# x by an identity product in PSUM, first scores on 256 tokens, other packing of score rounds, a new order

## The chip, the cores and the metric

The kernel runs on one core of one Trainium2 chip. The metric is the device time of one execution in microseconds; where several runs are shown, their median. TensorE is called PE here, VectorE DVE, ScalarE ACT, GpSimd POOL; SP only issues DMAs.

## The reference, cut to what matters

x has 2048 tokens of width 512. Attention with a compressive memory and a gated MLP follow each other twice, each with a layer norm ahead of it and x added behind it. Attention works in 4 segments of 512 tokens, on 32 heads of width 16: a causal softmax inside the segment, mixed by sigmoid(beta) with a read of a memory M that the segments before it have filled.

```python
def _A_ref(x, wq, wk, wv, wo, beta):
    ...
    for s in range(N):                      # 4 segments of 512 tokens
        p = _softmax(qs @ ks.T * scale + mask)
        a_dot = p @ vs
        num, den = phi(qs) @ M, phi(qs) @ z + 1e-6
        o = g * num / den + (1 - g) * a_dot
        M, z = M + phi(ks).T @ vs, z + sum(phi(ks))
    return o @ wo

def _B_ref(x, w_gate, w_up, w_down):        # width 1792
    return _gelu(x @ w_gate) * (x @ w_up) @ w_down

x = x + _A_ref(_layernorm(x), ...)
x = x + _B_ref(_layernorm(x), ...)
x = x + _A_ref(_layernorm(x), ...)
x = x + _B_ref(_layernorm(x), ...)
```

## The kernel before

**Units of work.** Two passes of four segments make eight units, k = 0 to 7. Each unit has an attention part (`Att`) and an MLP part (`Ffn`). A segment is four tiles of 128 tokens. Weights and x stay in SBUF; PSUM has eight banks of 512 columns.

**Attention of a unit.** Four tiles of x are normed: bn_stats and bn_aggr on DVE (L514, L522), the power -1/2 on POOL for all four tiles at once (L527, L532), the scaling to xn on DVE or POOL (L544). xn is transposed into xnT, for k = 0, 1, 2 by PE through PSUM (a "turn", L586, copied out at L461 or L462), otherwise by a DMA. Then q, k and v are projected, blocks of four matmuls of 512 columns (L476 or L471). The scores of a group of four head pairs b and of a half of them (par 0 or 1) are packed into rounds of 256 columns (`FULL`), nine rounds for each b, the fifth being shared by both halves (`PAIRED`). A round has matmuls of 64, 192 or 256 columns on row tiles (L938). Two rounds at a time fill two pairs of banks; ACT takes the exponential of a pair (L1396) into the buffer pt; POOL masks the diagonal blocks of a round (L1343, `DIAG` says how many 64-column blocks), the shared round is masked by DVE (L1353) or by POOL in halves (L1348). A "flush" (L954) multiplies the five rounds of a half with v on column tiles, 40 matmuls; DVE turns and scales its result (L971 to L986). k is also copied with half of the heads set to zero (kx, L417, L422), which the odd half needs.

**Memory and MLP.** phi of q and k go through ACT, POOL and DVE (L741, L764, L745); k's is transposed by DMA. The projection wo is 16 matmuls, and DVE adds its result to x in SBUF (L1027). The norm of the sum is turned by PE for k = 0, 1 and 7 (`BY_PE`). Then 14 gate blocks of four matmuls (`gate`), gelu on ACT, 14 blocks `up` with a product on DVE (L1092), and `down`, 14 matmuls for each of four tiles, added to x again.

**What sets the order.** All engines run an order that is written out when the program is built: `order` keeps a clock for every engine (`Clocks`, `Engine`), with a cost written beside each instruction, and picks the next instruction of PE by due times and of the others by slacks. The numbers of this choice stand in `POLICY`; `CHANGES`, which can replace them in each stretch of 20 us, is empty. Where no item is ready while scores are left, PE gets a product of a constant tile, `warm`, whose result nobody reads (L476 or L471), called filler here. Ahead of each turn of a norm in `BY_PE` stand two such products of half width:

```python
            fill = FILL if self.key in BY_PE else 0
            ops = [(Clocks.MM[512] / 2, whole(lambda: nc.tensor.matmul(
                ps()[:, half:L], lhsT=warm[:], rhs=wide[:, 0:2, :], start=True, stop=True)))] * fill
```

A matmul of 512 columns can be issued whole (`128*128`, L476) or as four of 128*32 on column tiles (L471, `product`). PE is thus in one of three modes, whole, rows (scores) and columns (flushes and what is issued between them); `product` stays in column mode where a flush is near, so as to change mode less.

**The head, written out by hand.** 15 products of `warm` (L349) run first. Four tiles of x are loaded, then on ACT's queue beta, broadcast to 128 partitions, and on SP's queue wk and wq in halves of 256 columns. The first norm is computed tile by tile (L1183 to L1193, L544) and turned (L596), ACT copies two turned tiles and DVE two (`first_turn`, L599, L601); ACT takes two exponentials of beta ahead of its copies (L1202, L1203). The first k and q blocks are computed in halves of 256 tokens (`first_k` L909, `first_q` L914), all four halves ahead of the first two score rounds.

**The end.** The last unit's `down` adds to x, and SP stores each tile.

## Time and profile before

| | us |
|---|---|
| median of 3 runs | 546.09 (545.96 to 546.21) |
| profiled execution | 545.75 |
| its span, first to last instruction | 544.0 |

The table of stages below is the answer on busy time by stretch: from and to in us, its length, and for each engine the busy us and the number of instructions; then the granted share of PE's clock and the share of the DMA engines.

```profile
0.00:14.00 14.00, 11.41 (x83) 5.79 (x85) 9.78 (x31) 8.30 (x16) 6.64 (x17) 1.00 0.83 251
14.00:34.00 20.00, 19.53 (x293) 10.20 (x296) 18.56 (x45) 19.79 (x29) 17.40 (x21) 1.00 0.27 74
68.00:136.00 68.00, 67.11 (x1236) 34.86 (x1243) 63.24 (x120) 60.15 (x74) 46.29 (x51) 1.00 0.25 53
476.00:544.00 68.00, 64.66 (x628) 33.67 (x624) 33.22 (x58) 13.36 (x20) 2.43 (x3) 0.99 0.05 17
```

The columns after the length are PE, PEld (weight loads, which run beside matmuls), DVE, ACT and POOL. A matmul's row is longer than the time by which it holds up the next one, so busy PE is read from the starts of its matmuls, not from the sum of its rows. In the two early stretches DVE and ACT are also nearly full; in the last one there are no scores left, and PE works alone but for evictions and products.

Some rows of groups that the text uses (line, engine, operation, out<-in, shapes, count, busy us and mean ns of one, idle time ahead of it and who ended it):

```profile
L1396 ACT ACTIVATE pt<-ps 128x1024 bf16<-128x1024 f32 x288 | 278.9, 1025 | 44.6 <-PE ps L938 41.1 <-POOL pt L1343 2.5 <-POOL kx L417 0.2
L1343 POOL TENSOR_SCALAR_AFFINE_SELECT pt<-pt 128x256 bf16<-128x256 bf16 x128 | 60.2, 483 | 51.4 <-ACT pt L1396 45.5 <-PE ps L938 4.7
L1343 POOL TENSOR_SCALAR_AFFINE_SELECT pt<-pt 128x512 bf16<-128x512 bf16 x64 | 47.7, 745 | 66.6 <-ACT pt L1396 66.5
L532 POOL TENSOR_TENSOR rs<-ve,mhalf 128x4 f32<-128x4 f32 x15 | 16.4, 1092 | 1.2
```

### The profile page before, as it was taken

What the parts mean: (1) busy time and instruction counts of PE and PEld (TensorE: products, weight loads), DVE (VectorE), ACT (ScalarE), POOL (GpSimd) and SP (SyncE); (2) the same over time, 40 slices, a digit from 0 to 9 for tenths busy, and PEclk for the clock granted to TensorE, in tenths of its full rate; (3) what the DMA queues carried; (4) which work ended last, traced back from release to release, by engine and by line L of the source; (5) the groups of instructions that cost most, each with busy time, mean ns of one, the idle gap of its engine ahead of it and who ended that gap; (6) DMA issues with size and microseconds to landing.
All of it is one profiled execution on the core that took longest, in us unless ns stands there. A gap on an engine that the chain in (4) does not pass through costs nothing.

```text
span 544.0 us, 21276 instructions
## 1 busy us (share of the span) xinstructions
PE 531.3 (98%) x9273; PEld 276.3 (51%) x9334; DVE 443.7 (82%) x816; ACT 434.7 (80%) x540; POOL 305.5 (56%) x359
## 2 busy tenths in 40 slices
PE   8999999999999999999999999999999999999997
PEld 4454555454545444554545555545465456555444
DVE  6998999799988999779987998889586797786342
ACT  5999989988898989989899798996879977920330
POOL 4898786369746788339993468716753265300000
PEclk9999999999999999999999999999999999999999
DMA  8406511610331123310312250221320114100001
GB/s 249 117 13 192 118 20 13 176 33 22 45 56 21 26 40 58 44 40 7 41 32 49 33 72 3 41 32 23 78 52 3 22 21 82 24 3 22 19 0 40
DMA packets 64926, 26.95 MB, mean 50 GB/s; under 512 B 49216, under 2 KB 64832, under 8 KB 64832
## 3 DMA queue, kind: packets, MB, share of 16 engines
q1 hardware_dynamic: 64400, 25.31, 22.6%
q8 instruction: 73, 1.20, 0.9%
q10 hardware_dynamic: 432, 0.27, 0.2%
q14 instruction: 21, 0.17, 0.1%
HBM read 9.71 MB, written 2.10 MB: 22 GB/s over the span
## 4 chain that ended last, share of the span: by engine, by line
PE 88%; DVE 7%; DMA 2%; issue 2%; ACT 0%; ACTq 0%; SPq 0%; DVEq 0%
PE ps L476 46%; PE ps L471 26%; PE ps L938 8%; PE ps L954 7%; DVE st L514 1%; DVE x_sb L1027 1%; DMA beta_bc<-in_A_beta_dram 1%; DVE byq L971 1%; PE ps L586 1%; DVE phiq L745 1%; PE ps L584 1%; DMA phik<-e 0%; DMA amT<-am 0%; DVE xn L544 0%; DVE e L764 0%
## 5 line engine op out<-in xcount | busy, mean ns | idle before, releaser
L1396 ACT ACTIVATE pt<-ps 128x1024 bf16<-128x1024 f32 x288 | 278.9, 1025 | 44.6 <-PE ps L938 41.1
L1343 POOL TENSOR_SCALAR_AFFINE_SELECT pt<-pt 128x256 bf16<-128x256 bf16 (+1 forms) x192 | 107.0, 571 | 118.0 <-ACT pt L1396 112.0
L1092 DVE TENSOR_TENSOR gel_sb<-gel_sb,ps 128x512 bf16<-128x512 bf16 x112 | 75.3, 682 | 33.9 <-PE ps L476 25.0
L476 PE MATMUL ps<-xnT,wu_sb 128*128 128x512 bf16 x287 | 66.8, 379 | 1.4 <-issue 1.1
L476 PE MATMUL ps<-xnT,wg_sb 128*128 128x512 bf16 x261 | 62.6, 379 | 0.9 <-issue 0.5
L764 POOL TENSOR_SCALAR e<-e 128x512 bf16<-128x512 bf16 x37 | 57.9, 1565 | 1.8 <-ACT e L741 0.7
L971 DVE STREAM_TRANSPOSE byq<-ps 128x512 f32<-128x512 f32 x64 | 45.0, 706 | 16.5 <-PE ps L954 15.9
L476 PE MATMUL ps<-wd_sb,gel_sb 128*128 128x512 bf16 (+1 forms) x293 | 56.8, 340 | 1.3 <-issue 1.0
L1348 POOL TENSOR_SCALAR_AFFINE_SELECT pt<-pt 64x1024 bf16<-64x1024 bf16 x40 | 47.8, 1196 | 15.0 <-ACT pt L1396 13.7
L1027 DVE TENSOR_TENSOR x_sb<-x_sb,ps 128x512 bf16<-128x512 bf16 (+1 forms) x68 | 42.8, 640 | 16.3 <-PE ps L476 14.7
L471 PE MATMUL ps<-wd_sb,gel_sb 128*32 128x512 bf16 (+1 forms) x792 | 47.1, 378 | 0.3 <-issue 0.3
L476 PEld LDWEIGHTS <-wu_sb 128*128 128x128 bf16 x301 | 28.2, 98 | 33.8 <-issue 0.7
L471 PE MATMUL ps<-xnT,wg_sb 128*32 128x512 bf16 x700 | 42.4, 380 | 0.0
L514 DVE BATCH_NORM_STATS2 st<-x_sb 128x6 f32<-128x512 bf16 x60 | 40.4, 674 | 0.4 <-DMA x_sb<-in_A_x_dram 0.3
L476 PEld LDWEIGHTS <-wg_sb 128*128 128x128 bf16 x273 | 25.3, 98 | 28.8 <-issue 0.2
L476 PEld LDWEIGHTS <-gel_sb 128*128 128x128 bf16 x306 | 28.3, 98 | 22.7 <-issue 1.1
L954 PE MATMUL ps<-pt,vaug 128*32 128x256 bf16 (+2 forms) x1344 | 34.6, 238 | 0.0
L417 POOL TENSOR_SCALAR kx<-kf,masks 128x512 bf16<-128x512 bf16 x20 | 33.5, 1678 | 1.2
L471 PE MATMUL ps<-xnT,wu_sb 128*32 128x512 bf16 x588 | 34.1, 379 | 0.0
L1151 ACT ACTIVATE gel_sb<-gel_sb 128x2048 bf16<-128x2048 bf16 (+1 forms) x21 | 33.2, 1643 | 0.0
L544 DVE TENSOR_SCALAR xn<-x_sb,mv,rs 128x512 bf16<-128x512 bf16 x58 | 31.3, 592 | 2.2 <-POOL rs L532 1.9
L954 PEld LDWEIGHTS <-vaug 128*32 128x32 bf16 x1344 | 27.8, 97 | 10.4 <-issue 2.2
(147 smaller groups left out, 883.6 us busy)
## 6 DMA issues: line engine op xcount, KB each, us to landing
vz<-vaug SPq DMA_DIRECT2D x14, 136.0 KB, 2.9
wg_sb<-in_B_w_gate_dram SPq DMA_DIRECT2D x8, 224.0 KB, 4.6
wu_sb<-in_B_w_up_dram SPq DMA_DIRECT2D x8, 224.0 KB, 4.3
wd_sb<-in_B_w_down_dram SPq DMA_DIRECT2D x7, 256.0 KB, 4.2
x_sb<-in_A_x_dram SPq DMA_DIRECT2D x3, 512.0 KB, 7.3
out_dram<-x_sb SPq DMA_DIRECT2D x12, 128.0 KB, 1.8
xnT<-xn SPq DMA_TRANSPOSE x40, 2.5
wk_sb<-in_A_wk_dram SPq DMA_DIRECT2D x2, 256.0 KB, 6.0
```

The lines of the kernel that those rows point to most:

```text
L471: nc.tensor.matmul(out[r], lhsT=lhsT[:, r], rhs=rhs, start=start, stop=stop, tile_position=(0, 32 * c))
L476: nc.tensor.matmul(out, lhsT=lhsT, rhs=rhs, start=start, stop=stop)
L514: nc.vector.bn_stats(out=self.st6[:, 0, :], in_=x_sb[:, self.tt0 + j, :])
L764: lambda eng: eng.tensor_scalar(out=e[0][:], in0=e[0][:], scalar1=1.0, scalar2=None, op0=ALU.min), summed)
L938: nc.tensor.matmul(ps_all[:, bank, o + c0:o + c0 + n], lhsT=lhsT, rhs=self.q[rows, b, q0:q0 + n], start=True, stop=True, tile_position=(32 ...
L954: nc.tensor.matmul(ps()[32 * j:32 * j + 32, q0:q0 + n], lhsT=va[:, ki * VW + g:ki * VW + g + 32], rhs=pt_all[:, places[i], j, c0:c0 + n], ...
L971: nc.vector.transpose(out=self.byq[:, par, :, :].rearrange("p a c -> p (a c)"), in_=ps()[:])
L1027: ck.dve.post(ck.made(), slack, (0.15 + 0.00104 * (c1 - c0), lambda: nc.vector.tensor_tensor(out=xt, in0=xt, in1=ps()[:, 0:c1 - c0], op=AL ...
L1092: ck.dve.post(ck.made(), NORMAL, (0.683, lambda: nc.vector.tensor_tensor(out=g, in0=g, in1=ps()[:], op=ALU.mult), lambda t: (ps.read(t), e ...
L1343: nc.gpsimd.affine_select(out=view, in_=view, pattern=[[0, 4], [0, n], [1, C]], compare_op=ALU.is_ge, fill=0.0, base=C, channel_multiplier=-1)
L1348: nc.gpsimd.affine_select(out=view, in_=view, pattern=[[0, 4 * TPS], [1, C]], compare_op=ALU.is_ge, fill=0.0, base=0, channel_multiplier=-1)
L1396: nc.scalar.activation(out=pt_all[:, s0:s0 + 2, 2 * p:2 * p + 2, :].rearrange("p r h c -> p h r c"), in_=ps_all[:, pair[0]:pair[1] + 1, :] ...
```

## The change

- **Order and policy.** `POLICY` has other values, and `CHANGES` now holds values for each of 28 stretches of 20 us; the planner's costs of DMA issues and POOL instructions are changed, and so the order of nearly everything is new. FILL is gone; `pol.fill`, which takes its place, is 0 everywhere. One more input norm (`pe_turns` 3 for 2) is turned by PE.
- **x in PSUM.** For units k < `pol.x_pe`, `wo` begins with a product of the identity and x, so that the sum stands in PSUM; bn_stats reads it there, and an eviction writes x.
- **Norm and gates.** The norm ahead of the MLP is scaled in two groups of two tiles; the first four gate blocks of each unit (`split`) are computed in halves of 256 tokens, the first half as soon as two tiles are turned. The first `wo` block (`wsplit`) is issued without its last matmul, which follows when the last attention tile is there.
- **Rounds.** `FULL` packs the first two rounds otherwise, `DIAG` is [2, 0, 0, 2] for [1, 1, 0, 2], and `ORDER` gives the rounds of each b another sequence; two rounds that need the same mask get it in one POOL instruction. In unit 0 two pairs of banks that lie side by side share one exponential (`join`), and evictions, gelus and products of neighbouring banks can be joined (`Mate`).
- **Head.** beta is loaded as one row and brought to all partitions by a product with ones; 13 products of `warm`; the first two score rounds need 256 tokens alone and are issued ahead of the second halves of q and k (`first_scores`).

```diff
-WARM = 15
+WARM = 13
...
-FULL = [[(0, 64, 256, 0)], [(1, 192, 64, 0), (0, 320, 192, 64)], [(1, 256, 256, 0)], [(3, 448, 64, 0), (2, 320, 192, 64)]]
-DIAG = [1, 1, 0, 2]
-SHARED = len(FULL)
+FULL = [[(1, 192, 64, 0), (0, 64, 192, 64)], [(0, 256, 256, 0)], [(1, 256, 256, 0)], [(3, 448, 64, 0), (2, 320, 192, 64)]]
+DIAG = [2, 0, 0, 2]
+ORDER = [[(1, 2, 0, 3), (1, 0, 3, 2)], [(1, 0, 3, 2), (0, 3, 1, 2)]]
...
+def turns_of(k, b):
+
+    if (k, b) == (0, 0):
+        return [(0, 0), (1, 0), (0, 1), (0, 2), (0, 3), None, (1, 1), (1, 2), (1, 3)]
+    one, two = ORDER[b % 2]
+    return [(0, n) for n in one] + [None] + [(1, n) for n in two]
...
-    flush_wait=31.348, piece_slack=5.108, kb_slack=25.115, mem_slack=-15.103, margin=2.314, qk_due=0.572,
+    x_pe=0, mates=0, split=4, wsplit=1, last_wait=56.902, join=1, fill=0, x_whole=0, hold=0, early=10.599,
+    starve=2.654, near=-3.158, cap=2, soon=12.345)
...
+    0: dict(flush_wait=48.203, piece_slack=4.818, kb_slack=8.912, mem_slack=-7.53, margin=4.263, qk_due=1.3,
...
+    2: dict(flush_wait=48.163, piece_slack=-3.804, kb_slack=8.4, mem_slack=-7.699, margin=3.439, qk_due=1.026,
...
-    beta_bc = cst.tile([P, H], BF16, name="beta_bc")
+    beta_row = cst.tile([1, H], BF16, name="beta_row")
...
-    nc.scalar.dma_start(out=beta_bc[:], in_=A_beta.partition_broadcast(P))
+    nc.scalar.dma_start(out=beta_row[:], in_=A_beta.partition_broadcast(1))
...
-            self.mv, self.n, self.left = None, 0, TPS
+            self.mv, self.rs, self.xnT, self.left = None, None, None, TPS
+            self.group = 2 if key[0] == "xnTf" else TPS
+            self.n = [0] * (TPS // self.group)
...
+                nc.gpsimd.tensor_tensor(out=self.rs[:, rows, :], in0=got[0], in1=mhalf[:, 0:self.group, :], op=ALU.pow)
+            ck.pool.post(ready, URGENT, (0.25, first, None), (0.41 + 0.16 * self.group, second, lambda t: ck.when(
+                self.free, lambda: self.start(max(t, ck.pe), rows))))
...
-            fill = FILL if self.key in BY_PE else 0
+            fill = pol.fill if self.key in BY_PE and self.key[1] < NK - 1 else 0
...
-                work = [(i + par * (SHARED + 1), self.vaug, *piece) for i, pieces in enumerate(FULL) for piece in pieces]
-                work += [(SHARED, vz, *piece) for piece in PAIRED]
+                turns = TURNS[k, b]
+                work = [(turns.index((par, n)), self.vaug, *piece) for n, pieces in enumerate(FULL) for piece in pieces]
+                work.sort(key=lambda w: w[2])
+                work += [(turns.index(None), vz, *piece) for piece in PAIRED]
...
+                inside = k < pol.x_pe
+                if inside:
+                    pairs = [(lambda: ident[:], lambda: x_sb[:, self.tt0 + j, :])] + pairs
+
+                def summed(t):
+                    ev["sum", k, j] = t
+
+                def added(t):
+                    summed(t)
+                    self.norm.stats(j, t)
+
+                def keep():
+
+                    both = Readers(ps, 2)
+                    self.norm.stats(j, ck.made(), ps, both.read)
+                    evict(both, lambda: x_sb[:, self.tt0 + j, :], lambda: ps()[:], summed, URGENT)
...
+                def second():
+                    items.append(Item(due - 0.5, lambda: ck.has(("aT", k, KT - 1), by=ck.pe - 0.1), ops[-1:], done,
+                                      kind="half", ps=ps, after=("aT", k, KT - 1)))
+
+                return Item(due, lambda: ("scores", k) in ev and soon(("aT", k), KT - 1), ops[:-1], second, kind="wo", ps=ps,
+                            after=("aT", k, KT - 2))
...
+                if ft >= pol.split:
+                    return Item(due, lambda: ck.has(("xnTf", k)) and clear(), dense(ps, pairs), done, kind="gate", ps=ps,
+                                after=("xnTf", k), mate=(("gate", k), ft))
+
+                def part(h):
+                    c = slice(L // 2 * h, L // 2 * (h + 1))
+                    return [(Clocks.MM[512] / 2, lambda i=i: product(
+                        ps()[:, c], wg_sb[:, i, ft * P:(ft + 1) * P], self.norm.xnT[:, i, c], i == 0, i == KT - 1))
+                        for i in range(KT)]
+
+                def second():
+                    items.append(Item(-0.9, lambda: ck.has(("xnTf", k)), part(1), done, kind="half", ps=ps, after=("xnTf", k)))
+
+                return Item(due, lambda: ck.has(("xnTf", k, 0), ("xnTf", k, 1)) and clear(), part(0), second, kind="gate",
+                            ps=ps, after=("xnTf", k, 1), mate=(("gate", k), ft))
...
-    n0.first_xn += [n0.normed(2, 2), n0.normed(3, 3)]
 
     a0 = att[0]
     a0.made()
     half = L // 2
-    n0.first_turn(0)
-    n0.first_turn(1)
-    n0.first_turn(2)
-    n0.first_turn(3)
+    n0.first_turn(0, nc.scalar)
+    n0.first_turn(1, nc.vector)
+    n0.first_xn += [n0.normed(2, 2), n0.normed(3, 3)]
+    beta_ps = ps_all[:, BANKS - 1, 0:H]
+    nc.tensor.matmul(beta_ps, lhsT=warm[0:1, :], rhs=beta_row[:], start=True, stop=True)
+    nc.scalar.activation(out=tmp_e, in_=beta_ps, func=ACT.Exp)
+    nc.scalar.activation(out=tmp_e2[:], in_=beta_ps, func=ACT.Exp, scale=-1.0)
     ps1 = ps_all[:, 1, :]
     a0.first_k(ps1, 0, half)
     nc.scalar.activation(out=a0.kf[:, 0, 0:half], in_=ps1[:, 0:half], func=ACT.Copy)
+    nc.vector.tensor_scalar(out=a0.kx[:, 0, 0:2, C:3 * C], in0=a0.kf[:, 0, 0:half].rearrange("p (t c) -> p t c", c=P),
+                            scalar1=masks[:, 1:2], scalar2=None, op0=ALU.mult)
     ps2 = ps_all[:, 2, :]
     a0.first_q(ps2, 0, half)
     nc.scalar.activation(out=a0.q[:, 0, 0:half], in_=ps2[:, 0:half], func=ACT.Copy)
-    ps3 = ps_all[:, 3, :]
-    a0.first_q(ps3, half, L)
-    nc.vector.tensor_copy(out=a0.q[:, 0, half:L], in_=ps3[:, half:L])
-    ps0 = ps_all[:, 0, :]
-    a0.first_k(ps0, half, L)
-    nc.scalar.activation(out=a0.kf[:, 0, half:L], in_=ps0[:, 0:half], func=ACT.Copy)
+    n0.first_turn(2, nc.vector)
+    n0.first_turn(3, nc.scalar)
     gate_constants()
-    ev["xnTa", 0] = 0.0
-    ev.update({("xnTa", 0, j): 0.0 for j in range(TPS)})
-    ck.pe, ck.act.free, ck.dve.free, ck.pool.free, ck.sp.free = 10.6, 11.1, 11.0, 8.1, 7.6
-    banks[0:4] = [10.8, 9.45, 9.9, 10.4]
-    ev["q", 0, 0] = 10.35
-    a0.n_qkv = 2
-    a0.k_done(0, None, 11.2)
+
...
+    def first_scores():
+
+        ck.pe, ck.act.free, ck.dve.free, ck.pool.free, ck.sp.free = 9.15, 9.6, 10.2, 8.1, 6.5
+        banks[:] = [1e9] * 4 + [8.5] * 4
+        score(2)
+        ps3 = ps_all[:, 3, :]
+        a0.first_q(ps3, half, L)
+        nc.vector.tensor_copy(out=a0.q[:, 0, half:L], in_=ps3[:, half:L])
+        ps0 = ps_all[:, 0, :]
+        a0.first_k(ps0, half, L)
+        nc.vector.tensor_copy(out=a0.kf[:, 0, half:L], in_=ps0[:, 0:half])
+        ck.pe, ck.dve.free, ck.mode = 10.5, 11.1, "whole"
+        banks[0:4] = [11.15, 8.75, 9.15, 10.72]
+        ev["xnTa", 0] = 0.0
+        ev.update({("xnTa", 0, j): 0.0 for j in range(TPS)})
+        ev["q", 0, 0] = 10.67
+        a0.n_qkv = 2
+        a0.k_done(0, None, 11.1)
...
+
+        n = [n for _, n, _ in marks]
+        if len(marks) == 2 and n[0] and n[0] == n[1]:
+            def both(t):
+                for _, _, done in marks:
+                    done.append(t)
+
+            ck.pool.post(at, NORMAL, (Port(0.18 + 0.49 * n[0]), lambda: mask(marks[0][0], n[0], 2), both))
+            return
...
+        joined = pol.join > (rounds[0][0] > 0) and pairs[1][0] == pairs[0][1] + 1
+        for p, got in enumerate([pairs[0] + pairs[1]] if joined else pairs):
```

The values in `CHANGES` that bear on the parts above: `x_pe` is 0 in `POLICY` and in stretches 0, 1, 6 to 10, it is 1 in 2 to 5, 18 and 23, and 2 in 19 and 20; `join`, `split`, `wsplit`, `pe_turns`, `fill` and `mates` are never changed.

495 lines of the change are left out of this document (359 added, 136 removed).

## The prediction

> **What bounds the kernel.** I read the page first: the shares of the engines and the chain that ended last.
>
> ```profile
> PE 531.3 (98%) x9273; PEld 276.3 (51%) x9334; DVE 443.7 (82%) x816; ACT 434.7 (80%) x540; POOL 305.5 (56%) x359
> ...
> PEclk9999999999999999999999999999999999999999
> ...
> PE 88%; DVE 7%; DMA 2%; issue 2%; ACT 0%; ACTq 0%; SPq 0%; DVEq 0%
> ```
>
> TensorE is taken 98% of the span, the chain lies on it for 88%, and its clock is full. So the time is what TensorE issues plus what it waits for, and I made an account of that. Then the timeline of PE, to turn matmuls into time. First, plain work in the last segment:
>
> ```profile
> 507.87 1.89 PE L476 MATMUL ps<-xnT,wg_sb 128*128 128x512 bf16 x8
> 509.60 1.89 PE L476 MATMUL ps<-xnT,wu_sb 128*128 128x512 bf16 x8
> ```
>
> One matmul lasts 379 ns by its row, but the next begins earlier: 8 of them advance the clock by 509.60 - 507.87 = 1.73 us, 216 ns each. The start-to-start times of the whole trace give 216 ns for 512 columns, 109 for 256 and 56 for 128; four 128*32 matmuls in column mode advance together, also 216 ns for 512 columns. A change of mode costs extra:
>
> ```profile
> 236.66 1.47 PE L471 MATMUL ps<-xnT,wu_sb 128*32 128x512 bf16 x24
> 238.07 0.40 PE L938 MATMUL ps<-q,kf 16*128 16x256 bf16 x12
> ```
>
> Six groups of four end at 236.66 + 6 x 0.216 = 237.96; the score rows begin at 238.07. Over all such pairs a switch costs 0.09 to 0.11 us, 0.10 in the mean. Put on the full list of instructions of the program before (a few matmul records are missing in the trace), this gives 502.0 us of streaming and 301 switches, 30.1 us. The first matmul is at 1.1 us, the last ends 3.3 us before the end of the span, so 544.0 - 1.1 - 3.3 - 532.1 = 7.5 us is waiting: 3.7 us before 11 us, and only **3.7-3.8 us** in the other 530. A faster VectorE or ScalarE has little to gain here; what can be gained is useless streaming. That is the third view, the timeline of PE in the hole between segment 0's output projection and its gates:
>
> ```profile
> 73.82 1.47 PE L471 MATMUL ps<-warm 128*32 128x512 bf16 x24
> ...
> 75.55 1.47 PE L476 MATMUL ps<-warm 128*128 128x512 bf16 x6
> ...
> 77.63 0.39 PE L584 MATMUL ps<-warm 128*128 128x256 bf16 x2
> ...
> 81.29 1.03 PE L476 MATMUL ps<-xnT,wg_sb 128*128 128x512 bf16 x3
> ```
>
> Products of `warm` are filler: the planner issues them where nothing real is ready, and L584 puts two before each turn. They look busy and are waiting.
>
> **Part by part**, from the instruction lists of both built programs (no time is in them), times the rows above.
>
> 1. *Filler.* Behind the head, before: 19 whole (4.10 us), 12 column groups (2.60), 24 halves of L584 (2.62), 9.3 us: 5 in the hole at 66 to 81 us, 2.8 at 126 to 137, 0.9 ahead of the last gates, 0.4 early, 0.2 near 110. After: 20 whole, 10 groups, no halves, 6.5 us: 1.5 early, 0.4 at 35, 1.3 and 1.1 in the two holes, 0.2, and a new 1.9 us near 260. **-2.83 us**, if nothing real waits in its place (rival A). What shortens the holes: gates 0 to 3 are computed on 256 tokens at a time, and the norm ahead of them is scaled in groups of two tiles. By rows, from the last attention tile turned (X): wo of two tiles, 8 matmuls and the sums (0.68 each), statistics (0.67 + 0.18), scale on POOL (1.04 for four; 0.71 and 0.80 for two in the head), xn behind all four statistics at X + 8.6, transposes, copies of 0.41: first gate half at X + 10.1. The list has 11.2 us of PE work there, filler counted. Before, X was 65.7 and the first gate 81.3, X + 15.6.
> 2. *Turns.* One more input norm is turned on PE: 16 transposes of 56 ns, **+0.90**, and four fewer DMA transposes.
> 3. *Gates in halves.* 128 products of 512 become 256 of 256: 128 x (2 x 109.3 - 216.3), **+0.30**; other small forms +0.08.
> 4. *Switches.* 301 become 295, fewer of whole-to-row and more of column-to-row: **-0.50**.
> 5. *Head.* beta now takes one descriptor and no longer holds ACT. In the page's chain the first piece is that DMA; the row of the wait is "ACT macc L1202: 1.2" on it, and the two copies of xnT follow at 7.37. Without it the first copy can go at 6.9, the second (now on DVE, 0.41) at 7.4 to 7.85. But wk lands at 1.70 + 5.7 = 7.4 and wq at 2.17 + 6.1 = 8.3, so the q half is at 8.35 to 8.8, its eviction (0.38, behind k's) to 9.4, two score rounds 9.45 to 9.8, the other four tiles' halves of q and k (8 x 0.109) to 10.9. Before, the same state was reached at 11.12: **-0.2**. ACT begins its exponentials some 1.3 us sooner, which helps only where PE waits for them. Two of 15 warm-up products go, off the path. The new product of beta stands in PE's queue ahead of the first k; what is queued behind it waits for a DMA, but 128 descriptors landed at 7.09, before 7.85, and one should not be later: 0.
> 6. *Identity product and moments in PSUM.* They are not in the program. `inside` asks `k < pol.x_pe` when the objects are built, in window 0, where x_pe is 0; the list has no product of `ident` with x_sb, no bn_stats on ps, and as many adds of x as before: 0. (Done, it would be 8 products, +1.7 us.)
> 7. *Packing and masks.* Score and flush matmuls have the same counts and sizes. 192 masks on POOL become 63 of twice the size and 2: 107.9 us of POOL become about 81 (483 ns at 256 elements, 745 at 512, hence an estimate of 1.27 us at 1024). Thirteen joined exponentials save some 0.2 us each on ACT, shorter gelus give 3 us back. DVE gets 10 more kx copies of 0.47. PE covers all this at 98%; uncovered it is rival B.
> 8. *Waits behind the head.* 3.7 us stay as they are. The lists cannot show them: between 0 and twice as much.
>
> Sum: -2.83 + 0.90 + 0.38 - 0.50 - 0.2 = **-2.25 us**. The profiled execution took 545.75 us (span 544.0), so 543.5; the median of the runs, 546.09, is 0.34 above it: **543.8 us**, -0.4%. A measurement of this kernel can tell about 0.2%, 1.1 us, from no change.
>
> **Rivals.**
>
> *A. The cover goes, the wait stays.* The filler becomes idle time, because xn comes no sooner. For it: xn has a median of 412 ns on DVE but up to 1290, with POOL busy beside it, and a mask of 1.27 us is the longest neighbour yet. Against: the spare 1.1 us of step 1. The sum is then 0.90 + 0.38 - 0.50 - 0.2 = +0.6: 546.7, no change that can be told. Chance 0.13. The Trainium skill, SBUF — State Buffer, "Who interferes with whom", says that VectorE's two-port forms and GpSimd exclude each other for a whole instruction; by that rule an xn can wait out a whole mask, twice in each hole: 4 x 1.27 us, most of what step 1 has to spare. The stretch from 412 to 1290 ns agrees.
>
> *B. Slower: flushes come too early.* The lists put the flush of odd heads 2.7 us (least) and 3.4 (median) of PE work behind its last score round; before 3.5 and 4.6. In the trace the last exponential of a round ends 2.05 us after its scores (9 in 10 under 2.19). Before, one or two masks (0.48, 0.75) came on top; now that last round needs none, which is why the margin, about 0.5 us, is no less. If an eviction of 0.62 us stands ahead of the exponentials on ACT, the flush is 0.12 late, 32 x 0.12 = 3.8 us: 547.6. It decides from 0.07 us each. Chance 0.08.
>
> *C. More waits go than I count.* Of PE's waits over 0.1 us that I can place in the trace, 0.7 us lies in the two holes and 0.4 at a turn of an input norm, ended by VectorE; if shorter holes and a freer POOL take two thirds of the 3.7 us, 541.3. The lists, which show no waits, speak neither for nor against it. Chance 0.17.
>
> *D. Clock.* The first warm-up products advance 427 ns each, and 216 from 3.9 us on; with 13 they would end near 5.1 us and PE would be idle for 1.5 us to 6.6, against 0.9 to 1.1 before. If half clock returned for some 3.4 us it would cost 1.7: 545.5. Chance 0.02. The Trainium skill, TensorE: Matmul & The Clock Gate, "What's actually happening", has the clock fall back after an idle window of about 3.4 us; by that rule 1.5 us is too short, and the trace, 0.999 granted through a hole of 0.9, agrees as far as it goes.
>
> **Numbers.** Forecast 0.60, around 543.8 (542.3 to 545.2); A 0.13, B 0.08, C 0.17, D 0.02. The range takes in most of C and A: 541.2 to 546.6. Faster by over 0.2% (under 545.0): forecast and C, 0.77; within: A and D, 0.15; slower: 0.08.
>
> **What would show it.** On the page after, PE stays at 98%, the group of `warm` at L817's place is gone, `warm` falls from 70 to 44 groups. First scores at 9.4 to 9.6 us. In the timeline, the first gate half follows the last filler of the first hole without idle time: if idle stands there, A. Waits of PE at the flush line on ACT of over 2 us in all: B. Total idle of PE behind the head, by the same account, 3.7: much less is C, much more refutes step 8, on which most hangs.

## The result, and the profile after

| kernel | median, us | executions | spread |
|---|---|---|---|
| before | 545.97 | 6 | 545.75 to 546.21 |
| changed | 547.76 | 6 | 546.54 to 548.64 |

The ratio is 1.0031, with an interval of 1.0018 to 1.0043. The forecast was 543.8, faster; the changed kernel is slower by 1.8 us. Its profiled execution took 548.33 us, its span is 546.6. Of its page, the lines that answer to those shown of before:

```profile
PE 538.9 (99%) x10268; PEld 291.5 (53%) x10268; DVE 454.9 (83%) x830; ACT 435.1 (80%) x534; POOL 273.8 (50%) x243
...
PEclk9999899999999999999999999999999999999999
...
PE 89%; DVE 8%; ACT 1%; issue 1%; DVEq 0%; ACTq 0%
```

The 8 in the row of the clock, from 55 to 68 us, is the first thing to look at. DVE has 11 us more work than before, POOL 32 less. The account of the prediction, made again for this trace:

| us | before | after |
|---|---|---|
| matmuls of the list | 502.0 | 500.1 |
| switches | 301, 30.1 | 295, 29.6 |
| waits before 11 us | 3.7 | 4.1 |
| waits behind 11 us | 3.7 | 8.7 |

The list gives back 2.4 us; the waits behind the head take 5.0. What a half clock costs counts as waiting in this account. By stretches of 20 us they are like those of before (differences of at most 0.7, either way) but for one, 40 to 60 us, with 3.4 instead of -0.1. The timeline of PE there, whose bracket gives the idle time before a group and what ended it:

```profile
54.68 0.41 PE L1172 MATMUL ps<-wd_sb 16*128 16x256 bf16 x20
55.02 0.40 PE L817 MATMUL ps<-ident,xn 128*128 128x128 bf16 x4
56.64 0.61 PE L817 MATMUL ps<-ident,xn 128*128 128x128 bf16 x8 [1.22 <-DVE vaug L678]
57.96 0.43 PE L817 MATMUL ps<-ident,xn 128*128 128x128 bf16 x4 [0.71 <-DVE xnT L678]
58.29 1.44 PE L695 MATMUL ps<-wv_sb,xnT 128*128 128x512 bf16 x3
```

These are the four turns of input norm 3 (the norm ahead of the attention of unit 3), which are new on PE. The second waits for DVE to copy a tile of v out of the PSUM bank that it takes, the fourth for DVE's copy of an earlier turn. Behind them three matmuls of 512 columns take 1.44 us. Three at 216 ns would take some 0.81 by the same rows (two starts and the 379 ns of the last): the clock is at half. The windows of the same stretch, with the granted clock behind the five busy times, first of before and then of the changed kernel:

```profile
50.00:58.00 8.00, 7.95 (x138) 3.83 (x138) 6.83 (x13) 7.77 (x9) 6.36 (x8) 1.00 0.65 204
```

```profile
50.00:58.00 8.00, 6.07 (x168) 3.80 (x166) 7.89 (x15) 7.01 (x9) 7.76 (x7) 1.00 0.61 212
58.00:64.00 6.00, 6.00 (x47) 2.32 (x50) 4.45 (x9) 4.07 (x5) 3.39 (x4) 0.72 0.00 1
```

The columns are PE, PEld, DVE, ACT, POOL. From 50 to 58 us PE fell from 7.95 to 6.07 us of work, and DVE rose from 6.83 to 7.89 of 8: in this stretch DVE is the bound. What it does, and POOL beside it (kx are the copies of k with half of the heads set to zero, called key copies below):

```profile
50.46 2.24 DVE L600 TENSOR_SCALAR kx<-kf,masks 128x512 bf16<-128x512 bf16 x4
...
53.85 2.14 DVE L775 TENSOR_SCALAR xn<-x_sb,mv,rs 128x512 bf16<-128x512 bf16 x3
55.91 0.67 DVE L678 CAST vaug<-ps 128x512 bf16<-128x512 f32 x1
56.51 1.07 DVE L600 TENSOR_SCALAR kx<-kf,masks 128x512 bf16<-128x512 bf16 x2
57.50 1.07 DVE L678 COPY xnT<-ps 128x512 bf16<-128x512 bf16 x3
```

```profile
51.39 1.16 POOL L1662 TENSOR_SCALAR_AFFINE_SELECT pt<-pt 128x1024 bf16<-128x1024 bf16 x1
52.55 2.12 POOL L775 TENSOR_SCALAR xn<-x_sb,mv,rs 128x512 bf16<-128x512 bf16 x1
54.64 1.21 POOL L1662 TENSOR_SCALAR_AFFINE_SELECT pt<-pt 128x1024 bf16<-128x1024 bf16 x1
```

Four key copies take 2.24 us, though three of them last 0.35 each. The fourth, alone:

```profile
51.49 1.21 DVE L600 TENSOR_SCALAR kx<-kf,masks 128x512 bf16<-128x512 bf16 x1
```

It starts 0.10 us behind a joined mask and ends 0.14 behind it. The last of the three xn does the same beside the next mask, 54.74 to 55.99. The experiments come back to this row.

### The profile page after: what moved, and what is told of

Same layout as the page of the kernel before. It is cut to its first block, busy times and chain, and to the rows that moved or that the text cites. A ratio compares the mean times of both kernels' runs of the same rounds, so it can differ in the third digit from the quotient of the medians.

```text
span 546.6 us, 23072 instructions
## 1 busy us (share of the span) xinstructions
PE 538.9 (99%) x10268; PEld 291.5 (53%) x10268; DVE 454.9 (83%) x830; ACT 435.1 (80%) x534; POOL 273.8 (50%) x243
## 4 chain that ended last, share of the span: by engine, by line
PE 89%; DVE 8%; ACT 1%; issue 1%; DVEq 0%; ACTq 0%
PE ps L695 38%; PE ps L690 34%; PE ps L1172 8%; PE ps L1190 6%; PE ps L817 1%; PE ps L532 1%; ACT pt L1730 1%; DVE byq L1207 1%; DVE kx L600 1%; DVE x_sb L1268 1%; DVE st L735 1%; DVE phiq L979 1%; DVE vaug L678 0%; DVE pt L1672 0%; DVE ab L1215 0%
## 5 line engine op out<-in xcount | busy, mean ns | idle before, releaser
L1730 ACT ACTIVATE pt<-ps 128x1024 bf16<-128x1024 f32 (+1 forms) x275 | 275.8, 1070 | 36.9 <-PE ps L1172 32.5
L1662 POOL TENSOR_SCALAR_AFFINE_SELECT pt<-pt 128x1024 bf16<-128x1024 bf16 (+1 forms) x65 | 78.4, 1206 | 101.0 <-ACT pt L1730 98.7
L695 PE MATMUL ps<-xnT,wg_sb 128*128 128x256 bf16 (+1 forms) x329 | 57.8, 324 | 0.0
L690 PE MATMUL ps<-xnT,wu_sb 128*32 128x512 bf16 x992 | 56.4, 379 | 0.0
L690 PE MATMUL ps<-xnT,wg_sb 128*32 128x512 bf16 (+1 forms) x988 | 49.6, 343 | 0.0
L695 PE MATMUL ps<-xnT,wu_sb 128*128 128x512 bf16 x200 | 46.7, 380 | 0.0
L690 PEld LDWEIGHTS <-wu_sb 128*32 128x32 bf16 x992 | 26.5, 97 | 24.4 <-issue 0.2
L1448 ACT ACTIVATE gel_sb<-gel_sb 128x1024 bf16<-128x1024 bf16 (+1 forms) x42 | 37.8, 983 | 0.0
L1190 PE MATMUL ps<-pt,vaug 128*32 128x192 bf16 (+2 forms) x1344 | 34.9, 238 | 0.0
L690 PEld LDWEIGHTS <-wg_sb 128*32 128x32 bf16 x988 | 24.8, 97 | 14.7 <-issue 0.6
L1190 PEld LDWEIGHTS <-vaug 128*32 128x32 bf16 x1344 | 27.7, 97 | 8.9 <-issue 3.4
```

The lines of the kernel that those rows point to most:

```text
L690: nc.tensor.matmul(out[r], lhsT=lhsT[:, r], rhs=rhs, start=start, stop=stop, tile_position=(0, 32 * c))
L695: nc.tensor.matmul(out, lhsT=lhsT, rhs=rhs, start=start, stop=stop)
L1190: nc.tensor.matmul(ps()[32 * j:32 * j + 32, q0:q0 + n], lhsT=va[:, ki * VW + g:ki * VW + g + 32], rhs=pt_all[:, places[i], j, c0:c0 + n], ...
L1662: nc.gpsimd.affine_select(out=view, in_=view, pattern=[[0, 4 * rounds], [0, n], [1, C]], compare_op=ALU.is_ge, fill=0.0, base=C, channel_m ...
L1730: nc.scalar.activation(out=pt_all[:, s0:s0 + 2, h0:h0 + len(got), :].rearrange("p r h c -> p h r c"), in_=ps_all[:, got[0]:got[-1] + 1, :] ...
```

## The experiments

Each kernel differs from the changed one (or, where its name begins with b, from before) as its diff says, and keeps the order of the instructions on each engine unless said otherwise. Ratios are to before on the same chip. "Rest" is PE's waiting behind 11 us by the account above, the cost of a half clock counted in: 3.7 before, 8.7 changed. The changed kernel's three executions at full clock take 547.0 us in the mean, its other three 548.4; the profiled one is of the latter.

### The turns of norm 3

**e1_fill_norm3.** Fillers stand where PE waits.

```diff
+            if self.key == ("xnTa", 3) and j in (0, 2):
+                ops += [(0.0, whole(lambda: nc.tensor.matmul(
+                    ps()[:, half:L], lhsT=warm[:], rhs=wide[:, 0:2, :], start=True, stop=True)))] * (12 if j == 0 else 7)
```

> The changed kernel with 12 half-width products of the constant tile behind the first turn of input norm 3 and 7 behind the third, in the free halves of those banks; nothing else in the order moves. Local theory (the turns of that norm wait 2.3 us for DVE at 55 to 58 us, and PE's idle time there lets the clock fall to half for 3.4 us): the clock stays full in every execution, the waits are filled but not shortened, and the slow executions of 548.3 come down by 1.5 us, to 546.8, with less spread. Spread theory (the new order loses a little everywhere, and the clock is a symptom): no change, or up to 2 us more for 2.1 us of added products.

Measured 547.59, 1.0032 (1.0019 to 1.0044); rest 5.9, of it 0.5 from 40 to 60 us; clock at 1.000 in all five executions, spread 547.46 to 548.02. So the fall of the clock follows from the idle time. The 546.8 that were expected did not come: the fillers cost what they hide, and this removes the spread, not the loss.

**e2_xn_dve.** The one xn of norm 3 that POOL makes goes to DVE.

```diff
-                            Port(2.05, True), lambda eng: made.append(self.normed(j, i, eng)), told)
+                            Port(2.05, True), lambda eng: made.append(self.normed(j, i, nc.vector if self.key == ("xnTa", 3) else eng)), told)
```

> The changed kernel with the one scaling of input norm 3 that POOL does (2.12 us at 52.6) moved to DVE at the same place; all other orders are the same. If DVE is late because its own scalings wait for POOL's (the three took 2.14 us where 1.2 are usual), PE's wait at the turns falls from 2.3 to about 1.3 us and the clock may stay: 545.5 to 546.5. If DVE is late because of its kx copies and evictions, it has 0.4 us more to do: 547.8 or a little more.

Measured 550.73, 1.0088 (1.0074 to 1.0102); rest 10.7. PE's waits from 40 to 66 us:

```profile
PE ps L817 <- DVE vaug L678: 1.6, 1, 1.6
PE ps L817 <- DVE xnT L678: 1.2, 1, 1.2
```

That is 3 us more than expected. Taking POOL's xn away does not free DVE; it has one more xn to do, and the clock stays at half for 6.83 us instead of 3.41. I took from this that POOL does not hold DVE at all. That was too much: the joined masks were still there, one of them (54.29 us, 1.20 long) beside the four xn (53.77 to 56.33).

**e3_turn_dma.** Norm 3 is turned by DMA, as in the kernel before; its transposes on PE and their copies are left out.

```diff
-                            Port(2.05, True), lambda eng: made.append(self.normed(j, i, eng)), told)
+                            Port(2.05, True), lambda eng: (made.append(self.normed(j, i, eng)), self.key == ("xnTa", 3) and
+                            nc.sync.dma_start_transpose(out=self.xnT[:, :, j * P:(j + 1) * P], in_=made[0][:])), told)
...
-            ops += [(Clocks.MM[128], whole(lambda kt=kt: nc.tensor.transpose(
+            by_dma = self.key == ("xnTa", 3)
+            ops += [(Clocks.MM[128], whole(lambda kt=kt: by_dma or nc.tensor.transpose(
```

> The changed kernel with input norm 3 turned by DMA, issued right behind each scaling, as in the kernel before; the 16 transposes and four copies out of PSUM are left out, all else keeps its order. Local theory: 0.9 us of PE work, the waits of 2.3 and the half clock of 1.5 go, at most 0.5 comes back because a DMA lands 2.5 us after its issue: 544 to 545. Spread theory: only the 0.9 goes, 546.9.

Measured 551.38, 1.0097 (1.0083 to 1.0111); rest 11.6. PE waits for the transpose instead:

```profile
PE ps L695 <- DMA xnT<-xn: 2.8, 3, 1.7
```

That is over 6 us more than the local theory expected. Taking the turn off PE does not bring the time back: at this place of the order, with nothing else moved, PE waits longer for the DMA than for DVE's copies.

**e4_kx_cost.** The builder's price of a key copy on DVE, 0.35, is set to 0.53, and the whole order follows from it anew.

```diff
-        ck.dve.post(ready, slack, (Port(0.35), vector(0, nc.vector), None),
-                    (Port(0.35), vector(1, nc.vector), told), taken=taken)
+        ck.dve.post(ready, slack, (Port(0.53), vector(0, nc.vector), None),
+                    (Port(0.53), vector(1, nc.vector), told), taken=taken)
```

> The changed kernel planned again with one cost of the planner mended: a kx copy on DVE counts 0.53 us, as the trace has it at 50 to 58 us, instead of 0.35. The PE work of the new order is 1.1 us more (530.9 for 529.7). If DVE was late because the planner took these copies for too short, waits behind the head go back to some 4 us: 544.5 to 545.5. If not, they stay near 8.7: 548.5 to 549.5.

Measured 553.82, 1.0149 (1.0133 to 1.0165); rest 12.4, spread over the span: above both ranges. One cost changed gives a whole new order, whose own waits hide what the edit itself does. After this I changed nothing that moves the order, but for e6.

**n1_kx_act, n2_kx_v_act, n3_kx_later.** Work of DVE ahead of the turns' copies goes to ACT: two key copies (n1); v's eviction too (n2); the same, with the key copies behind ACT's next exponential (n3).

```diff
   n1, n2 (masked_copies):
+            return lambda: scalar(which)() if 54.6 < ck.pe < 54.8 else eng.tensor_scalar(
   n3 (there, and behind the exponential):
+            return lambda: held.append(scalar(which)) if 54.6 < ck.pe < 54.8 else eng.tensor_scalar(
+                while held:
+                    held.pop(0)()
   n2, n3 (evict):
+        ck.dve.post(ck.made(), slack, (0.673, lambda: nc.scalar.activation(
+            out=dst(), in_=src(), func=ACT.Copy) if 54.3 < ck.pe < 54.4 else nc.vector.tensor_copy(out=dst(), in_=src()), end), taken=taken,
```

> The changed kernel, same order on every engine but for two of VectorE's key copies (the pair that runs there from 56.51 to 57.57 us, behind v's eviction and ahead of the copies of norm 3's turns), which ScalarE does in its own form between its eviction of v and the exponential of W_delta; the exponential that starts at 55.27 comes some 1.2 us later. Theory 'VectorE is out of throughput from 42 to 60 us': the copies of the turns start a microsecond earlier, the second wait in the turns (0.88 us at 57.03) goes, the first (1.39 at 55.2) stays, and with one piece of idle time left the clock should stay full: rest of the waits behind the head 6.0 to 7.0 instead of 8.7, time 546.2 (545.4 to 547.0), 1.0 to 2.0 below the changed kernel. Rival 'ScalarE and PE are as tight there': PE waits for the exponential or for norm 3's last copy instead, 0.9 us or more at a new place, and the time stays at 547.2 to 548.3.

> As the kernel above, and v's eviction (VectorE, 55.91 to 56.58), whose PSUM bank the second turn of norm 3 takes, goes to ScalarE as well, right behind its own v eviction at 54.24. Theory 'VectorE is out of throughput': the first wait (1.39 at 55.2) falls below 0.5 too, the clock stays full in every execution, rest of the waits 4.5 to 5.5, time 545.2 (544.5 to 546.2): what the sum of steps 1 to 7 had promised, less the other new waits. Rival: ScalarE, 1.8 us later with its exponential, makes PE wait as long: 547 to 548.5. Rival 'it is norm 3's normalised rows that come too late, not the banks': the first wait stays above 1 us with another name on it.

> As n2_kx_v_act, but ScalarE does the two key copies behind the exponential that starts at 55.27 instead of ahead of it, in the 1.3 us in which it idled in the changed kernel; only v's eviction (0.6 us) stands ahead of that exponential. In n2 PE's waits in this place were 0.4 to 0.6 for a normalised row and 1.1 to 1.2 for the late exponential, where n1 had one of 1.4 for the bank. Theory 'each of the three engines is within a few per cent of full from 50 to 58 us, so what is taken off one lands on the next, and only ScalarE's 1.3 idle us can be used': the wait for the exponential falls below 0.6, the rest of the waits to 5.7 to 6.3 (n1 and n2: 6.9), time 545.8 (545.2 to 546.5). Rival 'PE's waits there are set by the normalised rows alone': about 1.4 us of waits stay, 546.6.

| | us | ratio | rest | 40 to 60 us |
|---|---|---|---|---|
| n1 | 546.62 | 1.0008 (0.9999 to 1.0016) | 6.9 | 1.8 |
| n2 | 546.73 | 1.0010 (1.0001 to 1.0019) | 6.9 | 2.1 |
| n3 | 546.43 | 1.0009 (1.0000 to 1.0017) | 6.8 | 1.2 |

The clock stays at 0.999 or 1.000 in all 34 executions. n1 came out as expected, also in the wait that stays. In n2 that wait moved on, in the way of the rival:

```profile
PE ps L1174 <- ACT pt L1732: 1.1, 1, 1.1
PE ps L819 <- DVE xn L777: 0.4, 1, 0.4
```

n2 missed its 545.2. n3 was to save 0.9 over n2; by the medians, of two chips, it saved 0.3, by the ratios nothing that can be told. This relief of DVE is worth about 1.2 us, the clock's part included, and then stops; in the changed kernel ACT is busy 7.01 and POOL 7.76 of these 8 us, and what is left in n3 are waits for ACT (0.6) and for a row of xn (0.4).

### The joined masks and exponentials

**u1_exp_apart, u2_mask_apart, u3_mask_here.** The 13 joined exponentials are done in two parts (u1), the joined masks in two (u2), and only the three joined masks beside norm 3 in two (u3).

```diff
   u1 (exp):
+                for g in range(0, len(got), 2):
+                    nc.scalar.activation(
+                        out=pt_all[:, s0:s0 + 2, h0 + g:h0 + g + 2, :].rearrange("p r h c -> p h r c"),
+                        in_=ps_all[:, got[g]:got[g] + 2, :].rearrange("p h (r c) -> p h r c", r=2), func=ACT.Exp, scale=SCALE)
   u2 (post_masks):
-lambda: mask(marks[0][0], n[0], 2)
+lambda: [mask(s, n[0], 1) for s, _, _ in marks]
   u3 (post_masks):
+lambda: [mask(s, n[0], 1) for s, _, _ in marks] if 44 < ck.pe < 58 else mask(marks[0][0], n[0], 2)
```

> The changed kernel, same order on every engine, with its 13 joined exponentials (128x2048, 1.87 to 1.93 us) done as two of 128x1024 each (1.06 by the group's row), so the first half's bank comes free 0.9 us sooner and the second half some 0.2 later. Three of the joined ones stand at 48, 52 and 55 us, beside norm 3. If the joined form brings the scattered waits (theory 'join'), the rest of the waits falls by 0.5 us or more and the time by as much: 546.8 to 547.3. If not (theory 'order'), ScalarE has 2.5 us more work off the path and the time stays at 547.5 to 548.5.

> The changed kernel, same order on every engine, with its 65 joined masks on GpSimd (128x1024, 1.20 us) done as two of 128x512 each (0.745 in the kernel before): GpSimd gets some 19 us more work in the span and 1.5 us more between 46 and 58 us, where it is full. If the long masks bring the waits by holding VectorE's instructions (theory 'join'), time and waits fall: 546.5 to 547.3, and VectorE's key copies at 50.46 fall below 0.5 each. If GpSimd's share of the work is what counts there (theory 'all three engines full'), norm 3's rows come 1 us later and the time rises: 548.3 to 550.

> The changed kernel, same order, with only the three joined masks beside norm 3 (48.40, 51.39 and 54.64 us) done as two of half the size; the other 62 stay joined. Theory 'a mask holds a VectorE instruction that starts beside it until its own end, and only the stretch from 42 to 60 us has no slack': waits from 40 to 60 us fall from 3.4 to 1.0 us and the clock stays full, as with all masks apart, and the time is that of u2: 546.2 (545.8 to 546.8). Rival 'the gain of u2 is spread over the span': 547.2 or more.

| | us | ratio | rest | 40 to 60 us |
|---|---|---|---|---|
| u1 | 547.25 | 1.0029 (1.0017 to 1.0041) | 9.2 | 3.6 |
| u2 | 546.22 | 1.0006 (0.9997 to 1.0015) | 6.5 | 1.0 |
| u3 | 545.88 | 0.9995 (0.9986 to 1.0004) | 6.6 | 1.2 |

(The changed kernel has 63 masks of 128x1024 and two of half the size; so u3 leaves 60 joined.) u1 moved nothing that the intervals tell: its median lies in the range of 'join', but the ratio is that of the changed kernel, the rest did not fall, and the clock still falls in four of nine executions. u2 went the way of 'join', a little below its range. u3, which touches three masks, takes away the whole loss against the kernel before. Its profiled trace has the same matmuls in the same order as the changed kernel's: start by start it gains 2.17 us from 40 to 60 us, and 0.64 from 60 to 80, where the other is at half clock until 61.58; in no other stretch of 20 us do they differ by more than 0.31. DVE in u3:

```profile
50.34 1.74 DVE L600 TENSOR_SCALAR kx<-kf,masks 128x512 bf16<-128x512 bf16 x4
...
53.23 1.01 DVE L775 TENSOR_SCALAR xn<-x_sb,mv,rs 128x512 bf16<-128x512 bf16 x3
54.16 0.68 DVE L678 CAST vaug<-ps 128x512 bf16<-128x512 f32 x1
54.77 1.38 DVE L600 TENSOR_SCALAR kx<-kf,masks 128x512 bf16<-128x512 bf16 x2
56.07 1.07 DVE L678 COPY xnT<-ps 128x512 bf16<-128x512 bf16 x3
```

The four key copies go from 2.24 to 1.74, the three xn from 2.14 to 1.01. The eviction of v is done 1.7 us sooner and the first wait is gone. One is left, of PE from 40 to 66 us, for the copies that stand behind two key copies, which meet the new half masks:

```profile
PE ps L817 <- DVE xnT L678: 0.8, 1, 0.8
```

To see whether this is a rule I listed, over whole traces, each key copy or xn of DVE that starts while a mask of POOL has over 0.4 us to go, and took its end less the mask's:

```
kernel    cases   end of the DVE instruction behind the mask's end, ns
before    16      145 to 150
changed   10      144 to 147
u2        17      145 to 149
u3        11      144 to 148
```

No case is free. Such an instruction is held until the mask is done: an xn of 0.40 us alone took 1.25 beside a joined mask of 1.17 and 0.74 to 0.75 beside a half one of 0.67 to 0.71. The Trainium skill, SBUF — State Buffer, "Who interferes with whom", says that an instruction of VectorE in a two-port mode and one of GpSimd lock each other out for a whole instruction; for masks these 54 cases agree.

**w1_both, w2_both_nofill.** u2 and n3 together; and the same without fillers (next part).

```diff
+  w1: n3_kx_later with the masks of u2_mask_apart
+  w2: w1 without the product of warm in the idle case
```

> n3_kx_later (v's eviction and two key copies from VectorE to ScalarE) with all joined masks apart as in u2. In u2 one wait is left in norm 3's turns, 0.7 us for copies that stand behind two key copies, which n3 takes away; in n3 there were 0.4 for a normalised row and 0.6 for the exponential. If the two cures act on the same lateness, 0.5 to 0.8 us below u2: 545.5 (545.0 to 546.0). If each had its own wait, waits in the turns go to nothing and the time to 545.0. If ScalarE's exponential decides, 546.2, as u2.

> w1_both without the planner's 30 filler products (6.7 us of PE). n4 against n3 gained 0.3 us, so nearly all the filler that is left is cover: 545.2 (544.5 to 546.2), with 6 us more of waits. If the filler hid surplus that VectorE's lateness had eaten, 543 to 544.3.

w1 measured 547.20, 1.0023 (1.0013 to 1.0033), rest 7.9: a miss, slower than either cure alone. DVE now idles 1.06 us ahead of the turns' copies, and ACT, which got the work, is late:

```profile
PE ps L1176 <- ACT pt L1734: 1.1, 2, 0.6
```

w2 measured 545.90, 1.0001 (0.9991 to 1.0011), rest 12.6. So the two cures act on one lateness, and as far as these rows show the second only moves work to the next full engine. Of the 1.4 us by which w1's rest is above u2's, 0.8 lies from 40 to 80 us; the other 0.6 is scattered and I did not place it.

### The filler

**b1_nofill, b2_nofill_all** leave filler out of the kernel before, **e8_nofill** and **n4_later_nofill** out of the changed kernel and n3.

```diff
   b1, b2:
-            ops = [(Clocks.MM[512] / 2, whole(lambda: nc.tensor.matmul(
-                ps()[:, half:L], lhsT=warm[:], rhs=wide[:, 0:2, :], start=True, stop=True)))] * fill
+            ops = [(Clocks.MM[512] / 2, whole(lambda: None))] * fill
   b2 (in product, for column groups and whole ones):
+                if rhs is not wide:
   e8, n4:
-                product(ps(), warm[:], wide)
```

> The kernel before, same order, with only its 24 half-width fillers ahead of the turns of the first feed-forward norms left out (about 2.6 us of PE). It tries the first step of the prediction by itself. If those fillers were surplus there (the prediction's step 1), 543.4 (543.0 to 544.0). If they covered waits for the normalised rows and the turns' copies (rival A), PE waits there for 1.5 us or more, the granted clock may fall to one half behind them, and the time is 545.3 to 547.5. What the changed kernel showed in its turns of norm 3 speaks for the second: 546.

> The kernel before, same order, without any of its filler behind the head (24 halves and 31 whole or column groups, 9.5 us of PE). It tries what the filler of before was worth against the 6.5 us that are left after the change: if two thirds is surplus, as b1_nofill showed for the halves, 540 (539 to 541); the prediction's step 1 called it waiting in disguise, in which case at most the surplus of the holes (1.1 us and the halves' 1.8) goes: 543 to 544; and with the clock at half in the hole from 66 to 81 us, where 5 us of filler stand, 545 to 547.

> The changed kernel, same order, with all of the planner's 30 filler products left out (6.7 us of PE). It tries what the remaining filler is worth: if all surplus, 541 to 542; if all cover, PE's waits grow by 6.7 us and the time stays at 547 to 548, or goes above it where the clock falls to half in the holes. In b1_nofill two thirds of the removed filler became time saved, so by that theory 544 (543 to 546), with waits some 2 to 3 us longer and the clock's fall at 58 us as in the changed kernel.

> n3_kx_later without the planner's 30 filler products: the two edits together. If they add up, the changed kernel less 2.0 for n3 less what e8 saves: 542 to 543, below both kernels. If the clock falls in the holes that the filler had covered, 544 to 546.

| | left out, us | us | ratio | rest |
|---|---|---|---|---|
| b1 | 2.7 | 544.31 | 0.9969 (0.9958 to 0.9981) | 5.0 (before 3.7) |
| b2 | 9.5 | 545.04 | 0.9975 (0.9962 to 0.9988) | 13.1 |
| e8 | 6.7 | 548.33 | 1.0032 (1.0023 to 1.0042) | 13.7 (changed 8.7) |
| n4 | 6.7 | 546.12 | 1.0006 (0.9997 to 1.0015) | 12.9 (n3 6.8) |

I expected 546 for b1 and was wrong: of the 2.7 us of halves about 1.7 were surplus, and b1, below both kernels, has the lowest median of all that ran. e8 and n4 missed the other way (544, and 542 to 543, were expected): nearly all the filler that the change left is cover. At full clock e8 takes 547.0 in the mean of three executions, as the changed kernel does, with 6.7 us less to issue. Its rest, of an execution at full clock, grows by only 5.0 because the changed kernel's holds the half clock. w2 against w1 gains 1.3 of 6.7 us. Leaving out the other filler of before, too, gains nothing over b1. How much of it covers waits b2 does not tell, since it loses clock in each of its executions (0.991 to 0.997); its profiled one fell to half at 78.45 us for 6.83, and the rest of 13.1 holds that.

### The head, and the identity product

**e7_beta_wide.** beta is loaded as 128 rows again, and only the first is used.

```diff
-    beta_row = cst.tile([1, H], BF16, name="beta_row")
+    beta_row = cst.tile([P, H], BF16, name="beta_row")
-    nc.scalar.dma_start(out=beta_row[:], in_=A_beta.partition_broadcast(1))
+    nc.scalar.dma_start(out=beta_row[:], in_=A_beta.partition_broadcast(P))
```

> The changed kernel, same order, with beta loaded again as 128 rows (128 small descriptors) of which only the first row is used. It tries whether that load is what moved the arrival of the weights in the head: in the changed kernel the first half of W_k landed at 5.37 and W_q at 6.22 us, before at 7.43 and 8.28. Theory: the descriptors hold the weights up, W_k lands at 7.2 to 7.6 and W_q at 8.0 to 8.5, the first k product starts no earlier than that, and the head is 0 to 0.4 us longer: 547.8 (547.0 to 548.6), as the waits behind the head are not touched. Rival: something else in the head's queues moved them, and they land where they do in the changed kernel, with the same time.

Measured 548.77, 1.0042 (1.0027 to 1.0057). The issues of the first 12 us, with the median time to landing, of the changed kernel and of this one:

```profile
wk_sb<-in_A_wk_dram SPq DMA_DIRECT2D x2, 256.0 KB, 4.0
wq_sb<-in_A_wq_dram SPq DMA_DIRECT2D x2, 256.0 KB, 4.2
```

```profile
wk_sb<-in_A_wk_dram SPq DMA_DIRECT2D x2, 256.0 KB, 6.0
wq_sb<-in_A_wq_dram SPq DMA_DIRECT2D x2, 256.0 KB, 6.2
```

The 128 small descriptors held up the weights by 2 us. In the changed kernel the earlier weights buy nothing: the wait before 11 us is 4.0 to 4.1 in both, since its first k product waits for ACT until 8.01 us. So the 1 us by which this run is above the changed kernel, and above the range expected, is not in the head. The clock falls in four of six executions instead of three, and the profiled trace loses against the changed kernel's in a few more stretches, most (0.5) from 320 to 340 us; what waits there stays open.

**e6_x_pe.** The identity product and the moments in PSUM are really done, for units 0 and 1, in an order made anew.

```diff
-                inside = k < pol.x_pe
+                inside = k < 2
```

> The changed kernel with the identity product and the moments in PSUM really done for segments 0 and 1 (8 products, as the first line of the change says), planned anew. Its list has 533.5 us of PE work, filler and switches against 529.7: 1.7 for the products, the rest filler and switches of another plan. With the waits of the changed kernel 551.5 (550 to 553); e4, also planned anew, had 1.3 to 4 us more of waits than that of its order. If taking the add off VectorE's way to the statistics shortens the two holes as named in the change, 548 or less.

Measured 558.09, 1.0224 (1.0209 to 1.0240); rest 16.4. That is 6.6 us above what was expected. As with e4 the edit and a new order came together, so this does not price the product by itself.

## Why the prediction was wrong

**Steps 1 to 4 held.** The list and the switches gave -2.43; the terms said -2.05, and the two warm-ups less in the head (0.43) make up the rest to within 0.05. Step 1 named a condition, that nothing real waits in the filler's place. For the halves that went it was kept for the larger part (b1, in the order of before: about 1.7 of 2.7 us were surplus), and in the first hole the gate half follows the filler without idle time, 16 short score products between them:

```profile
79.79 1.46 PE L695 MATMUL ps<-warm 128*128 128x512 bf16 x6
81.18 0.40 PE L1172 MATMUL ps<-q,kf 16*128 16x64 bf16 x16
81.51 1.06 PE L690 MATMUL ps<-xnT,wg_sb 128*32 128x256 bf16 x32
```

**Step 5 was right where it looked.** First scores were to come at 9.4 to 9.6 us and the old state at 10.9; they came at 9.52 and 11.05, against 11.12 before:

```profile
4.07 2.77 PE L532 MATMUL ps<-warm 128*128 128x512 bf16 x6
...
8.01 0.60 PE L1143 MATMUL ps<-xnT,wk_sb 128*128 128x256 bf16 x4 [0.49 <-ACT tmp_e L1521]
...
9.52 0.41 PE L1172 MATMUL ps<-wd_sb 16*128 16x64 bf16 x16
...
11.05 1.03 PE L695 MATMUL ps<-xnT,wq_sb 128*128 128x512 bf16 x4
```

The gain is 0.07 and not 0.2. One reason given was wrong: wk landed at 5.4 us and not at 7.4, and PE waited for ACT's exponential of beta instead. Step 6 was right: no such product is in the trace.

**Step 7 is the step that failed**, "PE covers all this at 98%", with step 8, "3.7 us stay as they are", behind it: 8.7 were measured, which is the sign that the prediction itself named against step 8. 98% is a mean over the span. From 50 to 58 us the kernel before had PE at 7.95 of 8 and DVE at 6.83; what is new there, copies of the turns, more key copies on DVE and joined masks beside them, makes DVE the bound. The joined mask was costed as time of POOL (an estimate of 1.27; the median is 1.17), and there it is a saving: two halves take 1.33. Its price falls on DVE, 0.85 us for each instruction that it holds here. Three masks make the difference between 547.76 and 545.88 (changed and u3, on two chips; ratios 1.0031 and 0.9995). This price has two parts. The wait that it adds goes with u3. The fall of the clock behind it, some 1.4 us in the executions that have it, is that of rival D, which I gave 0.02 and looked for in the head. There it did not come: the profiled execution has full clock only from 6.97 us (before from 3.94), so its 13 warm-ups last until 6.84.

**Rival A had the mechanism and the wrong place.** It let an xn wait out a whole mask in the two holes. It does so there (an xn at 80.94 us takes 1.25), but the account shows from 60 to 80 us 0.77 of waits against 0.53, most of it the half clock until 61.58, and from 120 to 140 0.76 against 0.69: the filler left covers it. The prediction called a joined mask the longest neighbour yet, and it is not: the trace of before has 40 masks of the shared rounds, of 1.14 us in the median, and its xn of 1290 ns, at 348.34 us, ends 0.15 behind one of them. The question to ask of that row was where else DVE has no room, above all in a turn that the change makes new. Step 2 priced the turn at its 16 transposes, 0.90, and at none of its waits.

**Rival B came near the number by chance.** It said 547.6, by flushes that wait for ACT for over 2 us. In the changed kernel's list of PE's waits the flush line, L1190, stands with one wait of 0.2 us, and not for ACT.

**What stays open.** Of the 4.0 us between forecast and result the three masks explain about half: with them apart the kernel is level with before (0.9995), not 2 us below it. Even u3 has 6.6 us of rest against 3.7. Of this, 0.9 is the last wait at the turns, and 0.7 one flush at 406 us. The others are single waits of 0.25 to 0.4 us; neither joined masks (u2) nor joined exponentials (u1) bring them, which leaves the order itself, but no run shows that.

## What to carry to other kernels

Judge cover by stretch: before you cost an edit at nothing, read the windows of the place where it lands, for the engine that takes on the work and for the one that works beside it. An instruction made twice as long on POOL may be cheaper there and cost its whole length on DVE, so look in the trace for DVE instructions of several times their usual length and see what ends with them. In an order tuned to the last wait, a change is tried with the order held still; an edit that moves the whole order, as e4 and e6 do, says little about the change.

## What the runs showed of the hardware that was not expected

- **A clock that falls after two short waits.** In the profiled execution of the changed kernel the clock was full from 6.97 us for 51.20, at half from 58.17 for 3.41, and full again. In e2 and e3 it was full for 51.20 as well, then at half for 6.83; in b2 71.68 and 6.83. All are whole multiples of 3.413 us (15, 1, 2, 21). So windows of that length run by a phase of their own; the one from 54.76 to 58.17 held both waits of the turns, 1.93 us by the profile. A single wait of 1.2 (n1) left the clock alone in 12 executions. The same two waits do not always suffice: e8's profiled execution has them too (1.21 and 0.71) and keeps its clock, and the changed kernel falls in three of six, those three with spans of 546.6 to 546.9 against 544.8 to 545.5. That it depends on where the window lies fits this, but was not tried by itself. The Trainium skill, TensorE: Matmul & The Clock Gate, "What's actually happening", has the free-running window of 3413 ns, and the trace agrees; by its table the fall needs an idle window, and here one that was idle for a little over half, by the two waits, was enough.
- **A broadcast of 64 bytes to 128 partitions** delays weights on another queue by 2.0 us (e7).
- **The hold is exact**: 144 to 150 ns from the mask's end to that of the held key copy or xn, in 54 of 54 cases. POOL's own xn beside DVE's xn is not so strict: one DVE xn (53.85 us, 0.36 long) ran freely inside POOL's of 52.55 to 54.68, and the next was held to 0.14 behind its end.
